# Attention and gated linear unit: the scheduler's transfers gated, and one causal select per chunk for both heads

## The chip, the cores and the metric

One core of one Trainium2 chip. The metric is the device time of one execution in microseconds. Most executions of a kernel lie in a fast state; some take over 1.5% more than the fastest and are called slow. Verdicts use fast runs alone. The span of a profiled run is the time from its first to its last instruction.

## The reference

Eight sequences of 576 tokens, 8 heads of 64. Causal attention with a decay bias from `s`, then a gated linear unit: a causal convolution of five taps makes the gate, and two 512x512 products make value and output.

```python
scores = scale * q @ k.T + minimum(-(cum_i - cum_j), 0)   # cum = cumsum(relu(s)); causal mask
x      = softmax(scores) @ v                              # (B, S, 512)
gate   = sigmoid(sum_k conv_w[k] * x shifted by (4 - k) tokens)
out    = (gate * (x @ w_val)) @ w_out
```

## The kernel before

A chunk is two heads of one batch: 4 chunks a batch, 32 in all. For each: transposes of q and k on TensorE, copies to `QKT`, scores, three exponentials of 128x1024 on ScalarE into `P`, the causal select of the diagonal blocks on GpSimd, A x V on TensorE, normalisation on VectorE, a transpose to `xT`, four taps of the convolution, tanh, value product, glu. At the end of each batch come five output products, each copied from PSUM into an `ot` tile and stored.

No engine runs this in program order. A list scheduler inside the kernel decides, when the kernel is built, the order in which each engine's instructions are emitted, from a price in microseconds for every task, and each engine then works through its list in order: in the profile of before GpSimd stands idle for up to 3.3 us before a select, with other work behind it in its list. The prices are literals in the code. These parts matter here:

```python
plan = Plan(dict(P=3, gp=2, th=6, ot=3, qkf=3))         # buffers of each pool

def mask(n, hh):                                        # one head's four diagonal blocks
    d = slot["Pt", n][:, hh, 0:512].rearrange("k (g q) -> k g q", g=4)
    nc.gpsimd.affine_select(out=d, in_=d, pattern=[[0, 4], [1, 128]], compare_op=ALU.is_ge, fill=0.0, base=0,
                            channel_multiplier=-1)

def tap(e, n, sh):                                      # one tap: two instructions on GpSimd, one on VectorE
    ...
    if e == "POOL":
        nc.gpsimd.tensor_tensor(tmp[:, o:S], xs[:, 2 - sh + o:2 - sh + S], r.to_broadcast([128, S - o]), ALU.mult)
        nc.gpsimd.tensor_tensor(gp[:, o:S], tmp[:, o:S], gp[:, o:S] if o else xs[:, 2:], ALU.add)
    elif o:
        nc.vector.scalar_tensor_tensor(gp[:, o:S], slot["x", n][:, 0:S - o], r, gp[:, o:S], ALU.mult, ALU.add)
...
# prices: exponential 0.905, select 0.6 each, a tap 0.73 on VectorE or 2.25 on GpSimd
t = add("ACT", 0.905, n + 0.3 * i, lambda n=n, i=i: exps(n, i), [t], give=[("pair", ("s", n, i))])
es += [t] if i else [add("POOL", 0.6, n + due("mask") + 0.01 * hh, lambda n=n, hh=hh: mask(n, hh), [t])
                     for hh in range(2)]
...
t = add(("DVE", "POOL"), (0.73, 2.25), n + due("tap") + sh * due("dtap"), lambda e, n=n, sh=sh: tap(e, n, sh), ...)
```

Of the kernel before, what the change touches and what calls it, by code (L numbers as in the profile page):

```python
# [14 lines left out]
ALU = mybir.AluOpType  # L15
# [190 lines left out]
def pcol(kb, qb):  # L206
    if kb == qb:
        return kb * 128
    if qb == 4:
# [16 lines left out]
DUE = dict(w=-69.33, lwv=-4.26, lwo=-2.61, cwv=56.85, cwo=86.75, av=-11.07, norm=-74.98, xt=-16.64,  # L226
           xe=-86.49, tap=14.23, dtap=-1.47, tanh=-72.16, val=7.76, dval=0.88, out=11.28, dout=0.61,
           oute=87.55, qt=-4.79, qe=133.25, tt=-0.4, te=-149.08, s4=-20.03, vp=-7.1, cast=76.15, lqk=-1.56,
           mask=-123.76, lv=-49.38, av_e=7.71, av_l=6.68, cast_e=-31.51, cast_l=0.54, dout_e=-1.01,
           dout_l=-28.82, dtap_e=-7.57, dtap_l=16.17, dval_e=0.26, dval_l=0.84, lqk_e=-7.13, lqk_l=48.32,  # L230
           lv_e=98.37, lv_l=-92.01, mask_e=11.67, mask_l=11.41, norm_e=50.24, norm_l=38.99, out_e=0.39,
           out_l=42.92, oute_e=70.67, oute_l=-23.24, qe_e=-66.52, qe_l=-3.56, qt_e=4.39, qt_l=0.95,
           s4_e=8.96, s4_l=-14.16, tanh_e=58.9, tanh_l=56.45, tap_e=3.56, tap_l=-27.97, te_e=47.36,
           te_l=62.72, tt_e=19.75, tt_l=0.79, val_e=-3.44, val_l=-1.96, vp_e=-68.8, vp_l=29.32, xe_e=13.94,
           xe_l=0.22, xt_e=-5.82, xt_l=-13.61)


def due_of(b, name):
# [5 lines left out]
STAY = (0.1, 54.75)  # L244

CHOICE = dict(vp0="0100",
              cast="12200210",
              wts="00",
              te="10001100",
              qe="10100010000000001000100000100010",  # L250
              xe="00100010001000010000000000010010",
              tap="00000000100000000000001000000000000000010000100000000000000010000000000000001000001000001000100000000010000010010010001101110000",
              oute="1000001110101000010100010100011010000010")


class Plan:
# [22 lines left out]
    def run(self):  # L279
        engs = ["SP", "POOL", "PE", "ACT", "DVE"]  # L280
        free = {k: [(0.0, i) for i in range(n)] for k, n in self.bufs.items()}
        bank = [0.0] * 8
# [30 lines left out]
        while len(self.order) < len(self.tasks):  # L313
            started, later = False, []
            for e in engs:
# [36 lines left out]
                if e == "SP":  # L352
                    idle_at[e] = now + 0.06
                    dma_free = max(dma_free, now + 1.2) + us
                    t["done"] = dma_free + 0.8
                else:
                    idle_at[e] = t["done"] = now + us
# [21 lines left out]
def main_path(ctx, tc, q, k, v, s, moe_w_val, moe_conv_w, moe_w_out, out, okcnt):  # L379
# [9 lines left out]
    plan = Plan(dict(P=3, gp=2, th=6, ot=3, qkf=3))  # L389
# [81 lines left out]
    t = add("DVE", 0.65, -8, relu, [t_s])  # L471
    t = add("DVE", 1.3, -8, total, [t])
    t = add("DVE", 0.75, -8, centre, [t])
# [20 lines left out]
    t = add("SP", 0.3, -8.95, lambda: nc.sync.dma_start(out=cw, in_=moe_conv_w))  # L494
    t = add("PE", 0.3, -6, conv_T, [t], take=[("bank", "cw")])
# [11 lines left out]
    t_cw = add("DVE", 1.2, -6, ratios, [t], give=[("bank", "cw")])  # L507
# [9 lines left out]
    def cast_qk(eng, b, which, hs, f):  # L517
        eng(qkbs[which][b % 2].rearrange("p j (h d) -> p h j d", h=8)[:, hs],  # L518
                        f.rearrange("p h (j d) -> p h j d", j=4))
# [76 lines left out]
    def mask(n, hh):  # L596
        d = slot["Pt", n][:, hh, 0:512].rearrange("k (g q) -> k g q", g=4)
        nc.gpsimd.affine_select(out=d, in_=d, pattern=[[0, 4], [1, 128]], compare_op=ALU.is_ge, fill=0.0, base=0,  # L598
                                channel_multiplier=-1)
# [82 lines left out]
    for b in range(B):  # L682
# [4 lines left out]
        if b == 0:  # L687
            t_tl = add("SP", 1.45, -8.4, lambda: load_tail(0))
            t_tail = T["tailc", 0] = add("DVE", 0.45, -6, lambda: nc.vector.tensor_copy(tailbs[0], tails[0]), [t_tl])
            for p in range(4):  # L690
                for wh in range(2):
# [3 lines left out]
                    t = add("SP", 0.82, -8.5 + 0.5 * p + wh * 0.01, ld)  # L695
# [178 lines left out]
```

## Time and profile before

| | before |
|---|---|
| time, median of the 3 fast runs (range) | 211.16 us (209.36 to 211.21) |
| span of the profiled run | 209.3 us |
| first exponential of batch 1 | 31.8 us |
| last tap on GpSimd ends / TensorE ends / last copy ends | 195.8 / 201.8 / 204.0 us |

The prediction below shows the busy shares, the stretches, GpSimd's waits and the end. The groups of GpSimd's selects and tap halves are the ones to compare with the prices. They are from the view of groups by line; after the bar stand the busy time in us and the mean of one in ns, then the idle time before them:

```profile
L598 POOL TENSOR_SCALAR_AFFINE_SELECT P<-P 128x512 bf16<-128x512 bf16 x64 | 39.6, 640 | 11.3 <-ACT P L592 11.1
L644 POOL TENSOR_TENSOR tmp<-xT,ratio 128x576 f32<-128x576 bf16 (+3 forms) x18 | 20.6, 1142 | 1.0 <-ACT xT L635 0.5 <-DVE xT L635 0.2
L645 POOL TENSOR_TENSOR gp<-tmp,gp 128x573 f32<-128x573 f32 (+2 forms) x11 | 15.7, 1428 | 3.1 <-DVE gp L647 2.3
L645 POOL TENSOR_TENSOR gp<-tmp,xT 128x576 f32<-128x576 f32 x7 | 9.7, 1379 | 0.5
```

A select costs 0.64 us against a price of 0.6: right. A tap pair costs (20.6 + 15.7 + 9.7) / 18 = 2.56 us against 2.25: 0.3 too cheap, 18 times. The chain that ended last, by engine, has no GpSimd compute in it:

```profile
DVE 27%; ACT 24%; PE 23%; DMA 8%; issue 8%; SPq 7%; ACTq 0%; DVEq 0%
```

### The profile page before, as it was taken

The page shows a single profiled execution, that of the slowest core. Times are in us where ns is not written, and L with a number is a line of the kernel's source. Part 1 is how long each engine was busy: PE and PEld are TensorE (multiplying, and loading weights), DVE is VectorE, ACT ScalarE, POOL GpSimd, SP SyncE. Part 2 cuts the span into 40 slices and gives each one's busy share as a digit, 9 for nine tenths or more (in the row PEclk, how much of TensorE's full clock was granted, in tenths as well). Part 3 has the DMA queues.
Part 4 walks back from the last instruction along what each step waited for, and adds up shares of the span by engine and source line. Part 5 has one row for each costly group of instructions (what it writes and reads, how often), then busy time and mean ns, then how long its engine had stood idle before and what let it go on. Part 6 is the DMA issues. An engine that isn't in the chain of part 4 may idle for free.

```text
span 209.3 us, 6007 instructions
## 1 busy us (share of the span) xinstructions
PE 175.4 (84%) x2392; PEld 119.4 (57%) x2411; DVE 178.0 (85%) x311; ACT 163.1 (78%) x205; POOL 161.9 (77%) x179
## 2 busy tenths in 40 slices
PE   1697885999969998689899799989899999979950
PEld 0455763475736766367665567565576556645620
DVE  3847969999888998669999999999999998999810
ACT  3279497778999899987996998799987998553330
POOL 4276486499959998999589999967975899999300
PEclk9999797599999999999999999999999999999995
DMA  4999999997999699999999821951149220222551
GB/s 147 238 279 288 361 147 216 354 271 207 244 281 323 138 319 221 323 297 226 222 383 307 190 107 25 184 147 49 54 110 219 81 77 1 99 104 75 180 180 61
DMA packets 69230, 40.48 MB, mean 193 GB/s; under 512 B 47109, under 2 KB 63493, under 8 KB 69194
## 3 DMA queue, kind: packets, MB, share of 16 engines
q1 hardware_dynamic: 69194, 40.01, 72.7%
q8 instruction: 21, 0.34, 0.7%
q14 instruction: 15, 0.12, 0.2%
HBM read 30.57 MB, written 9.44 MB: 191 GB/s over the span
## 4 chain that ended last, share of the span: by engine, by line
DVE 27%; ACT 24%; PE 23%; DMA 8%; issue 8%; SPq 7%; ACTq 0%; DVEq 0%
ACT P L592 13%; DVE gp L647 9%; PE banks L660 8%; DMA qkf<-in_moe_w_val_dram 6%; PE banks L672 6%; DVE xn L623 4%; PE banks L613 4%; ACT QKT L561 4%; ACT th L653 4%; DVE glu L666 3%; DVE gp L649 3%; PE banks L566 3%; SPq L515 3%; SPq L534 2%; ACT ot L677 2%
## 5 line engine op out<-in xcount | busy, mean ns | idle before, releaser
L592 ACT ACTIVATE P<-banks 128x1024 bf16<-128x1024 f32 x96 | 94.8, 1039 | 11.8 <-PE banks L566 9.9
L647 DVE SCALAR_TENSOR_TENSOR gp<-banks,ratio,gp 128x574 f32<-128x574 bf16 (+2 forms) x85 | 67.5, 804 | 2.4 <-POOL gp L645 1.7
L598 POOL TENSOR_SCALAR_AFFINE_SELECT P<-P 128x512 bf16<-128x512 bf16 x64 | 39.6, 640 | 11.3 <-ACT P L592 11.1
L566 PE MATMUL banks<-QKT 64*128 64x128 bf16 (+4 forms) x576 | 38.9, 249 | 8.8 <-ACT P L592 5.6
L660 PE MATMUL banks<-xT,wv 128*128 128x288 bf16 x256 | 41.7, 294 | 2.1 <-DVE glu L666 0.9
L672 PE MATMUL banks<-wo,glu 128*128 128x512 bf16 x141 | 38.3, 379 | 2.5 <-ACT QKT L561 0.8
L528 POOL TENSOR_TENSOR Vp<-vst,w 128x650 bf16<-128x650 f32 x29 | 37.6, 1316 | 1.3 <-DMA vst<-in_v_dram 1.3
L613 PE MATMUL banks<-Vp,P 128*128 128x65 bf16 x960 | 37.3, 198 | 1.3 <-ACT P L592 1.2
L613 PEld LDWEIGHTS <-P 128*128 128x128 bf16 x960 | 35.3, 101 | 5.4 <-issue 2.1
L566 PEld LDWEIGHTS <-QKT 64*128 64x128 bf16 x576 | 20.1, 97 | 27.0 <-issue 20.6
L653 ACT ACTIVATE th<-gp,halfw 128x576 f32<-128x576 f32 x32 | 25.2, 793 | 7.1 <-DVE gp L647 3.6
L660 PEld LDWEIGHTS <-wv 128*128 128x128 bf16 x256 | 22.8, 99 | 13.9 <-issue 6.1
L666 DVE SCALAR_TENSOR_TENSOR glu<-th,banks 128x288 bf16<-128x288 f32 x64 | 28.0, 445 | 1.1 <-PE banks L660 1.0
L623 DVE TENSOR_TENSOR xn<-banks,recs 128x640 bf16<-128x640 f32 x32 | 26.2, 818 | 0.3
L561 ACT COPY QKT<-banks 128x1024 bf16<-128x1024 bf16 x25 | 25.3, 1049 | 1.2 <-PE banks L557 1.1
L677 ACT COPY ot<-banks 128x512 f32<-128x512 f32 (+1 forms) x26 | 15.2, 587 | 11.4 <-PE banks L672 6.9
L672 PEld LDWEIGHTS <-glu 128*128 128x128 bf16 x160 | 14.6, 97 | 15.5 <-issue 2.7
L649 DVE SCALAR_TENSOR_TENSOR gp<-xT,ratio,banks 128x576 f32<-128x576 bf16 x25 | 20.1, 809 | 1.6 <-ACT xT L635 0.9
L644 POOL TENSOR_TENSOR tmp<-xT,ratio 128x576 f32<-128x576 bf16 (+3 forms) x18 | 20.6, 1142 | 1.0 <-ACT xT L635 0.5
L645 POOL TENSOR_TENSOR gp<-tmp,gp 128x573 f32<-128x573 f32 (+2 forms) x11 | 15.7, 1428 | 3.1 <-DVE gp L647 2.3
L631 PE MATMUL banks<-ident,xn 128*128 128x128 bf16 x160 | 14.2, 220 | 2.9 <-DVE xn L623 1.2
L518 POOL CAST qb<-qkf 128x2048 bf16<-128x2048 f32 x7 | 13.2, 1890 | 2.2 <-DMA qkf<-in_q_dram 2.2
(63 smaller groups left out, 169.2 us busy)
## 6 DMA issues: line engine op xcount, KB each, us to landing
out_dram<-ot SPq DMA_DIRECT2D x32, 256.0 KB, 2.9
qkf<-in_q_dram SPq DMA_DIRECT2D x7, 1024.0 KB, 8.5
qkf<-in_k_dram SPq DMA_DIRECT2D x7, 1024.0 KB, 9.9
vst<-in_v_dram SPq DMA_DIRECT2D x28, 256.0 KB, 5.4
vst<-in_v_dram SPq DMA_DIRECT2D x15, 128.0 KB, 4.0
first<-in_q_dram SPq DMA_DIRECT2D x4, 256.0 KB, 3.4
first<-in_k_dram SPq DMA_DIRECT2D x4, 256.0 KB, 3.4
tail<-in_q_dram SPq DMA_DIRECT2D x8, 128.0 KB, 8.7
```

Source lines behind the costliest of these rows:

```text
L528: eng.tensor_tensor(Vps[b % 2][:, :, h], vst[:, :, h], w[:, :, b * 8 + 2 * p:b * 8 + 2 * p + 2].unsqueeze(3).to_broadcast([128, NKB, 2, 65 ...
L561: copy[e](QKTs[b % 2][:, :, p, 0:512].rearrange("d w (x j) -> d w x j", j=4), slot["qt", b, p].rearrange("d w (j x) -> d w x j", j=4))
L566: nc.tensor.matmul(ps[:, hh, c0:c0 + nq], QKTs[b % 2][r, 1, p, k0:k0 + 128], QKTs[b % 2][r, 0, p, q0:q0 + nq], **kw)
L592: nc.scalar.activation(out=slot["Pt", n][:, :, step * 512:(step + 1) * 512], in_=slot["s", n, step], func=AF.Exp, scale=0.125)
L598: nc.gpsimd.affine_select(out=d, in_=d, pattern=[[0, 4], [1, 128]], compare_op=ALU.is_ge, fill=0.0, base=0, channel_multiplier=-1)
L613: nc.tensor.matmul(ps[:, hh, qb * 65:qb * 65 + 65], lhsT, Vps[b % 2][:, kb, 2 * p + hh, :], start=(kb == 0), stop=(kb == qb))
L623: nc.vector.tensor_tensor(xns[b % 2][:, :, p * 128:(p + 1) * 128].rearrange("t g (h d) -> t h g d", h=2), pv[:, :, :, 0:64], recs[:, n].un ...
L647: nc.vector.scalar_tensor_tensor(gp[:, o:S], slot["x", n][:, 0:S - o], r, gp[:, o:S], ALU.mult, ALU.add)
L653: nc.scalar.activation(out=th, in_=slot["g", n], func=AF.Tanh, scale=halfw[:, n % 4, :])
L660: nc.tensor.matmul(ps, wv[:, dc, c * 128:(c + 1) * 128], xTs[b % 2][:, dc, 2 + o:290 + o], start=(dc == 0), stop=(dc == 3))
L666: nc.vector.scalar_tensor_tensor(glus[b % 2][:, c, o], slot["t", n][:, o], 1.0, slot["v", n, hf], ALU.add, ALU.mult)
L672: nc.tensor.matmul(ps, glus[b % 2][:, c, WIN[i]:WIN[i] + 128], wo[:, c, :], start=(c == 0), stop=(c == 3))
```

## The change

Two changes of the kernel and one of the scheduler's picture. One select of 1024 elements for both heads, priced at 0.75 us, takes the place of two of 512. `ot` gets five buffers in place of three. In the scheduler, a transfer may be issued no sooner than 11.48 us before the queue is thought free ("gating"; nothing on the chip waits for it). Then the keys (the scheduler's priorities) and engine choices were searched anew, so the order on all engines is another one.

```diff
-STAY = (0.1, 54.75)
-CHOICE = dict(vp0="0100", cast="12200210", ... )
+STAY = (1.35, 151.9)
+BEHIND = 11.48
+CHOICE = dict(tailc="2", vp0="1100", cast="00112001", ... )        # and all of DUE
 ...
                 if e == "SP":
-                    idle_at[e] = now + 0.06
                     dma_free = max(dma_free, now + 1.2) + us
+                    idle_at[e] = max(now + 0.06, dma_free - BEHIND)
 ...
-    plan = Plan(dict(P=3, gp=2, th=6, ot=3, qkf=3))
+    plan = Plan(dict(P=3, gp=2, th=6, ot=5, qkf=3))
 ...
-    def mask(n, hh):
-        d = slot["Pt", n][:, hh, 0:512].rearrange("k (g q) -> k g q", g=4)
-        nc.gpsimd.affine_select(out=d, in_=d, pattern=[[0, 4], [1, 128]], compare_op=ALU.is_ge, fill=0.0, base=0,
+    def mask(n):
+        d = slot["Pt", n][:, :, 0:512].rearrange("k h (g q) -> k h g q", g=4)
+        nc.gpsimd.affine_select(out=d, in_=d, pattern=[[0, 2], [0, 4], [1, 128]], compare_op=ALU.is_ge, fill=0.0, base=0,
                                 channel_multiplier=-1)
 ...
-                es += [t] if i else [add("POOL", 0.6, n + due("mask") + 0.01 * hh, lambda n=n, hh=hh: mask(n, hh), [t])
-                                     for hh in range(2)]
+                es += [t] if i else [add("POOL", 0.75, n + due("mask"), lambda n=n: mask(n), [t])]
```

The rest of the diff gives the first batch's loads, casts and transposes keys of their own in place of fixed ones.

More of the change, by code (lines that the diff above doesn't have):

```diff
@@ L222 @@
 NEG = -30000.0
-DUE = dict(w=-69.33, lwv=-4.26, lwo=-2.61, cwv=56.85, cwo=86.75, av=-11.07, norm=-74.98, xt=-16.64,
-           xe=-86.49, tap=14.23, dtap=-1.47, tanh=-72.16, val=7.76, dval=0.88, out=11.28, dout=0.61,
-           oute=87.55, qt=-4.79, qe=133.25, tt=-0.4, te=-149.08, s4=-20.03, vp=-7.1, cast=76.15, lqk=-1.56,
-           mask=-123.76, lv=-49.38, av_e=7.71, av_l=6.68, cast_e=-31.51, cast_l=0.54, dout_e=-1.01,
-           dout_l=-28.82, dtap_e=-7.57, dtap_l=16.17, dval_e=0.26, dval_l=0.84, lqk_e=-7.13, lqk_l=48.32,
-           lv_e=98.37, lv_l=-92.01, mask_e=11.67, mask_l=11.41, norm_e=50.24, norm_l=38.99, out_e=0.39,
-           out_l=42.92, oute_e=70.67, oute_l=-23.24, qe_e=-66.52, qe_l=-3.56, qt_e=4.39, qt_l=0.95,
-           s4_e=8.96, s4_l=-14.16, tanh_e=58.9, tanh_l=56.45, tap_e=3.56, tap_l=-27.97, te_e=47.36,
-           te_l=62.72, tt_e=19.75, tt_l=0.79, val_e=-3.44, val_l=-1.96, vp_e=-68.8, vp_l=29.32, xe_e=13.94,
-           xe_l=0.22, xt_e=-5.82, xt_l=-13.61)
+DUE = dict(w=-179.07, lwv=6.9, lwo=25.99, cwv=119.71, cwo=21.81, av=-67.91, norm=-106.36, xt=-83.29,
+           xe=-39.43, tap=73.53, dtap=-12.21, tanh=-21.14, val=7.28, dval=1.38, out=12.56, dout=0.92,
+           oute=44.7, qt=-5.37, qe=224.11, tt=0.85, te=-141.54, s4=-66.86, vp=-112.81, cast=107.85,
+           lqk=56.02, mask=-117.33, lv=13.25, av_e=68.91, av_l=-46.36, cast_e=-153.69, cast_l=-53.98,
+           dout_e=-12.2, dout_l=-66.84, dtap_e=-10.04, dtap_l=-64.5, dval_e=14.84, dval_l=-0.73,
+           lqk_e=-53.46, lqk_l=16.33, lv_e=84.68, lv_l=-81.16, mask_e=2.46, mask_l=30.46, norm_e=62.66,
+           norm_l=45.33, out_e=82.66, out_l=-73.32, oute_e=83.06, oute_l=-53.09, qe_e=-68.49, qe_l=46.96,
+           qt_e=-24.08, qt_l=3.94, s4_e=27.55, s4_l=-86.7, tanh_e=20.1, tanh_l=94.17, tap_e=-15.62,
+           tap_l=-2.33, te_e=-55.59, te_l=-34.48, tt_e=-48.5, tt_l=-36.85, val_e=-96.42, val_l=2.31,
+           vp_e=-46.58, vp_l=160.49, xe_e=32.24, xe_l=-1.61, xt_e=14.3, xt_l=-78.88, sd=-18.85, lcw=-44.05,
+           cvt=23.68, rat=-67.55, lt0=-98.57, tailc0=29.75, lq0=-12.67, lq0d=2.97, cast0=-5.61,
+           cast0d=127.18, lv0=-3.45, lv0d=2.76, vp0=32.35, vp0d=-5.83, tt0=62.96, te0=134.74, qt0=19.06,
+           qe0=-26.31, q0d=25.23)
@@ L238, in due_of @@
 def due_of(b, name):
     return DUE[name] + (DUE[name + "_e"] if b < 2 else DUE[name + "_l"] if b > 5 else 0)
-STAY = (0.1, 54.75)
-CHOICE = dict(vp0="0100",
-              cast="12200210",
-              wts="00",
-              te="10001100",
-              qe="10100010000000001000100000100010",
-              xe="00100010001000010000000000010010",
-              tap="00000000100000000000001000000000000000010000100000000000000010000000000000001000001000001000100000000010000010010010001101110000",
-              oute="1000001110101000010100010100011010000010")
+STAY = (1.35, 151.9)
@@ L256 @@
+BEHIND = 11.48
+CHOICE = dict(tailc="2",
+              vp0="1100",
+              cast="00112001",
+              wts="00",
+              te="00000100",
+              qe="01110110001000001001110000100100",
+              xe="01111000001011110000000100100111",
+              tap="00000000100001000000000100010000010000001100000000000010100000001000011000000010000100010000010010000110000100000100010010110000",
+              oute="0010011001000000110010100000000010001100")
 class Plan:
@@ L469, in decay_T @@
             nc.tensor.transpose(pt[:, i, :], cum[:, WIN[i]:WIN[i] + 128], identf)
-    t = add("DVE", 0.65, -8, relu, [t_s])
-    t = add("DVE", 1.3, -8, total, [t])
-    t = add("DVE", 0.75, -8, centre, [t])
+    t = add("DVE", 0.65, DUE["sd"], relu, [t_s])
+    t = add("DVE", 1.3, DUE["sd"], total, [t])
+    t = add("DVE", 0.75, DUE["sd"], centre, [t])
     t = add("PE", 1.2, DUE["w"], decay_T, [t], take=[("bank", "w")])
@@ L492, in conv_T @@
             nc.tensor.transpose(pt[:, c, :], cw[:, c * 128:(c + 1) * 128], identf[0:5, 0:5])
-    t = add("SP", 0.3, -8.95, lambda: nc.sync.dma_start(out=cw, in_=moe_conv_w))
-    t = add("PE", 0.3, -6, conv_T, [t], take=[("bank", "cw")])
+    t = add("SP", 0.3, DUE["lcw"], lambda: nc.sync.dma_start(out=cw, in_=moe_conv_w))
+    t = add("PE", 0.3, DUE["cvt"], conv_T, [t], take=[("bank", "cw")])
     def ratios():
@@ L505, in ratios @@
         nc.vector.tensor_scalar(ok[:, NS * NKB * 2:], sq, 1e20, None, ALU.is_le)
-    t_cw = add("DVE", 1.2, -6, ratios, [t], give=[("bank", "cw")])
+    t_cw = add("DVE", 1.2, DUE["rat"], ratios, [t], give=[("bank", "cw")])
     T = {}
@@ L687, in main_path @@
         if b == 0:
-            t_tl = add("SP", 1.45, -8.4, lambda: load_tail(0))
-            t_tail = T["tailc", 0] = add("DVE", 0.45, -6, lambda: nc.vector.tensor_copy(tailbs[0], tails[0]), [t_tl])
+            t_tl = add("SP", 1.45, DUE["lt0"], lambda: load_tail(0))
+            t_tail = T["tailc", 0] = add(("DVE", "ACT", "POOL"), (0.45, 0.48, 0.7), DUE["tailc0"], lambda e: copy[e](
+                tailbs[0], tails[0]), [t_tl], pick=("tailc", 0))
             for p in range(4):
@@ L694, in ld @@
                         dma_qk(0, wh, HP[p], f)
-                    t = add("SP", 0.82, -8.5 + 0.5 * p + wh * 0.01, ld)
-                    T["cast", 0, wh, p] = add(("DVE", "ACT", "POOL"), (0.32, 0.5, 0.8), p - 9, lambda e, p=p, wh=wh: cast_qk(
+                    t = add("SP", 0.82, DUE["lq0"] + DUE["lq0d"] * p + wh * 0.01, ld)
+                    T["cast", 0, wh, p] = add(("DVE", "ACT", "POOL"), (0.32, 0.5, 0.8), DUE["cast0"] + p * DUE["cast0d"], lambda e, p=p, wh=wh: cast_qk(
                         copy[e], 0, wh, HP[p], slot["f", 0, wh, p]), [t], pick=("cast", 2 * p + wh))
-                t = add("SP", 1.45, -8.3 + 0.5 * p, lambda p=p: load_v_pair(p))
-                T["vp", 0, p] = add(("DVE", "POOL"), (0.85, 1.25), p - 2, lambda e, p=p: vprime(
+                t = add("SP", 1.45, DUE["lv0"] + DUE["lv0d"] * p, lambda p=p: load_v_pair(p))
+                T["vp", 0, p] = add(("DVE", "POOL"), (0.85, 1.25), DUE["vp0"] + p * DUE["vp0d"], lambda e, p=p: vprime(
                     nc.vector if e == "DVE" else nc.gpsimd, 0, p), [t, t_w], pick=("vp0", p))
@@ L722, in main_path @@
         old_s = ([T.get(("s4", b - 2, 3))] + [T.get(("s", n0 - 8 + p, i)) for p in range(4) for i in range(3)])
-        t = T["tt", b] = add("PE", 0.25, n0 + due("tt") if b else -6.5, lambda b=b: tail_T(b), [t_tail] + old_s,
+        t = T["tt", b] = add("PE", 0.25, n0 + due("tt") if b else DUE["tt0"], lambda b=b: tail_T(b), [t_tail] + old_s,
                              take=[("bank", ("tt", b))])
-        t_te = add(("ACT", "DVE"), (0.49, 0.6), n0 + due("te") if b else -6.3, lambda e, b=b: tail_evac(e, b), [t],
+        t_te = add(("ACT", "DVE"), (0.49, 0.6), n0 + due("te") if b else DUE["te0"], lambda e, b=b: tail_evac(e, b), [t],
                    give=[("bank", ("tt", b))], pick=("te", b))
         for p in range(4):
-            t = T["qt", b, p] = add("PE", 0.45, n0 + p + due("qt") if b else p - 6.9, lambda b=b, p=p: qk_T(b, p),
+            t = T["qt", b, p] = add("PE", 0.45, n0 + p + due("qt") if b else DUE["qt0"] + p * DUE["q0d"], lambda b=b, p=p: qk_T(b, p),
                                     [T["cast", b, 0, p], T["cast", b, 1, p]] + old_s, take=[("bank", ("qt", b, p))])
-            T["qe", b, p] = add(("ACT", "DVE"), (0.9, 1.15), n0 + p + due("qe") if b else p - 6.8,
+            T["qe", b, p] = add(("ACT", "DVE"), (0.9, 1.15), n0 + p + due("qe") if b else DUE["qe0"] + p * DUE["q0d"],
                                 lambda e, b=b, p=p: qk_evac(e, b, p), [t], give=[("bank", ("qt", b, p))], pick=("qe", n0 + p))
```

## The prediction

> **What bounds the kernel now.** I read the page's busy shares first, then the table of stretches, the groups, the waits, the time-ordered view of GpSimd and of the last microseconds.
>
> The busy shares say that no engine is the bound alone:
>
> ```profile
> PE 175.4 (84%) x2392; PEld 119.4 (57%) x2411; DVE 178.0 (85%) x311; ACT 163.1 (78%) x205; POOL 161.9 (77%) x179
> ```
>
> The table of three stretches (start-up, middle, tail) shows where the remaining idle time lies: columns are PE, PEld, DVE, ACT, POOL busy us with counts, then clock, DMA share, GB/s.
>
> ```profile
> 0.00:40.00 40.00, 27.42 (x341) 19.59 (x341) 29.13 (x49) 26.29 (x35) 23.87 (x41) 0.89 0.97 249
> 40.00:180.00 140.00, 127.47 (x1905) 87.83 (x1921) 130.46 (x230) 127.33 (x156) 123.16 (x127) 1.00 0.75 192
> 180.00:209.00 29.00, 20.52 (x154) 11.98 (x152) 18.39 (x34) 9.46 (x15) 14.91 (x12) 0.93 0.36 125
> ```
>
> In the middle 140 us DVE is 93% busy, PE and ACT 91%, GpSimd 88%: four engines in one pipeline, each nearly full. Work taken from one and given to another pays only if the receiver has room. GpSimd has the most, and the view of waits says for what it stands still:
>
> ```profile
> POOL P L598 <- ACT P L592: 11.1, 11, 3.3
> POOL P L603 <- ACT P L578: 7.3, 5, 2.5
> ```
>
> These are the causal selects that come before the exponentials have delivered; they were put early in GpSimd's order.
>
> The end of the run, in order of time, is a shortage of buffers. Columns: start, duration, engine, line, what, and idle time before it with its releaser:
>
> ```profile
> 197.74 4.05 PE L672 MATMUL banks<-wo,glu 128*128 128x512 bf16 x17
> ...
> 201.08 0.59 ACT L677 COPY ot<-banks 128x512 f32<-128x512 f32 x1 [1.26 <-DMA out_dram<-ot]
> 203.44 0.59 ACT L677 COPY ot<-banks 128x512 f32<-128x512 f32 x1 [1.77 <-DMA out_dram<-ot]
> ```
>
> TensorE is done at 201.79, but the last two copies out of PSUM wait for a store to free one of three `ot` buffers; the last copy ends at 204.03.
>
> **What the Trainium skill says.** First, "GPSIMD Engine Reference", section 3.1: a GpSimd core runs a software loop whose bound is the number of elements, plus a dispatch for each instruction. The trace agrees for the select: 128 elements a partition take 0.31 us, 512 take 0.63, so about 0.84 ns for each element more. Second, "TensorE: Matmul & The Clock Gate", Architectural detail: ScalarE, VectorE and GpSimd are strict FIFO. So a kernel's emitted order is what counts, and a late GpSimd instruction delays all behind it; nothing in the trace contradicts that. Third, "DMA: Bandwidth & Descriptors", section on the SWDGE path: a wait for a semaphore happens on the issuing sequencer before dispatch, not in the DMA engines. The trace shows the same side of it: one queue on SyncE issues all, one after another, 0.4 to 0.7 us each from 0.81 to 16.5 us, and later a group of five loads takes 6.67 us to issue. Fourth, "SBUF — State Buffer", Who interferes with whom: a VectorE instruction in a two-port mode and GpSimd block each other. One case fits it: a GpSimd tap half that takes 1.38 us on average took 2.06 beside VectorE's 128x2048 weight cast.
>
> **The change part by part.** The kernel is emitted by a small list scheduler at build time. "Gating" changes only that scheduler's picture of the transfer queue (it no longer believes that it can issue every 0.06 us without limit); no wait is added on the chip. With it come new priorities and new engine choices, so the whole order moves. I counted instructions of each kind in both orders and multiplied by the mean durations of the groups.
>
> VectorE: 5 more QKT copies (1.217 us each, +6.1), 2 fewer small ones (0.42, -0.8), 3 fewer output copies (0.68, -2.1), 8 fewer xT copies (0.451, -3.6), 7 fewer taps (0.805, -5.6), 1 fewer Vp product (-0.8), casts about level. Sum -6.8: 178.0 becomes 171.
>
> ScalarE: 5 fewer QKT copies (1.049, -5.2), 2 more small ones (+1.2), 1 more cast (+0.6), 3 more output copies (+1.8), 8 more xT copies (0.664, +5.3). Sum +3.7: 163.1 becomes 167.
>
> GpSimd: 64 selects of 512 elements become 32 of 1024. A pair took 1.23 us back to back, so 64 cost 39.4. One of 1024 by the slope above is 0.63 + 512 x 0.84 ns = 1.06 us, 32 cost 34: -5.4. The scheduler is told 0.75 us; the trace gives me no reason to believe that, since only the fixed 0.2 us is saved, not half. Tap pairs rise from 18 to 25; a pair is 1.14 + 1.42 us: +17.9. One Vp product more (+1.3), casts net one fewer (-0.6). Sum +13.2: 161.9 becomes 175.
>
> TensorE: the same instructions, 175.4.
>
> The four together go from 678 to 688 us. So the gain cannot come from less work; it must come from less waiting.
>
> On the path that sets the end: **the tail.** The pool of `ot` buffers grows from 3 to 5, so the last copy can start at about 201.85 and end at 202.44 in place of 204.03: -1.6 us, the one item I am sure of.
>
> **The head.** Before, the first q/k and v loads alternate; after, all q/k of the first batch come first and the v loads behind them. Exponentials of batch 0 can follow each other with fewer gaps (ScalarE idles 4.4 of the 20 us from 10 to 30). But the first exponential gets no earlier (the tail loads come first now), and batch 1 waits for the same bytes: DMA share is 1.03 and 1.08 in these two slices. I give it -1 us.
>
> **GpSimd's line.** From the first select of batch 1 (at 33.65 us before) GpSimd has, before: 12 casts x 1.85, 28 products x 1.26, 7 small selects x 0.62, 5 tail casts x 0.57, 17 tap pairs x 2.62, 56 selects x 0.615 = 143.7 us (start to start durations). It ends its last tap at 195.77, so it idled 18.4 us. After: seven tap pairs more (+18.3) and 28 selects x 1.07 for 56 x 0.615 (-4.5): 157.5 us. With the same start its last tap ends at 191.2 plus its idle time, then tanh, glu, the last 20 output matmuls, a copy and a store: 195.77 to 209.3 is 13.5 us before, 11.9 with the buffers. Time over span is 1.7 us (211.03 against 209.3). So the time is at least 33.7 + 157.5 + 11.9 + 1.7 = 204.8 us plus GpSimd's idle time after batch 1 starts. An engine with 10 us more to do than its planner believes runs late, and a late engine seldom waits: I take 3 us of idle. That makes **207.8 us**.
>
> **The rivals.** One: GpSimd becomes the bound and makes others wait. For it: the sum above, 28 selects each 0.3 us dearer than the scheduler believes (8.9 us), and the matmuls that need the masked P. If 7 us of idle remain, the time is 212, no gain. Against it: the search that chose the new order may have had slack there, and batch 7 has less left on GpSimd (21 us of work from its first select, against 31.5). Two: VectorE was the real bound at 93%, its 6.8 us come off, and a better order of transfers closes gaps as well: 211.2 - 1.6 - 1 - 5 = 203.6. Against it: VectorE's relief is GpSimd's load. Three: the select of 1024 elements really costs 0.75 us; then GpSimd has 149 us after batch 1 and is no bound, 204 to 206. The 512-element group speaks against it. Four: transfers are hidden anyway (their share falls to 0.1 to 0.7 after 120 us) and their new order does nothing; then only tail and balance remain, about 209.
>
> **Range and chances.** The rivals span 203.6 to 212 and the runs before themselves 209.4 to 211.2. I set 203 to 213. Faster by 2% needs below 206.9; it needs rival two or three, or nearly no idle on GpSimd: 0.40. Within 2%: 0.54. Slower: 0.06, if GpSimd's lateness runs through everything.
>
> **What would show it.** Selects: a group of 32 with a mean of 1.03 to 1.10 us. GpSimd busy 173 to 177, VectorE 170 to 173, ScalarE 165 to 168. GpSimd's wait for the exponentials falls from 18 us to below 8. More of TensorE's and ScalarE's waits name GpSimd. The last copies wait for TensorE, none for a store. The middle stretch shows GpSimd at 94% or more. I am wrong if GpSimd still waits over 10 us for exponentials while the time falls below 206 (then batch 1 starts earlier, or the select is cheap), or if GpSimd is busy all through and the time is above 213.

## The result

| | before | after |
|---|---|---|
| time, median of 4 (range; 212.93 was a slow run) | 211.19 us (209.36 to 212.93) | 217.0 us (216.85 to 217.32) |
| span of the profiled run | 209.3 us | 215.1 us |

The ratio is 1.0307 (95% interval 1.0241 to 1.0373): slower by 3.1%. Ratios here are the mean time of one kernel's fast runs over that of the other's of the same rounds, so not quite the ratio of the medians.

Busy shares and chain of the kernel after. The forecasts of busy time came right (GpSimd 173 to 177, VectorE 170 to 173, ScalarE 165 to 168), and GpSimd, absent from the chain before, is now its largest part:

```profile
PE 176.6 (82%) x2394; PEld 120.2 (56%) x2411; DVE 172.8 (80%) x295; ACT 166.0 (77%) x214; POOL 177.0 (82%) x161
...
POOL 31%; PE 20%; DVE 13%; issue 13%; ACT 12%; SPq 4%; DMA 3%; POOLq 0%; DVEq 0%; ACTq 0%
```

GpSimd's groups of after. The select is 1.10 us, as forecast, not 0.75; 25 tap pairs cost (28.6 + 26.8 + 7.2) / 25 = 2.50 us each, not 2.25:

```profile
L604 POOL TENSOR_SCALAR_AFFINE_SELECT P<-P 128x1024 bf16<-128x1024 bf16 x32 | 35.1, 1099 | 5.1 <-ACT P L598 4.8
L650 POOL TENSOR_TENSOR tmp<-xT,ratio 128x574 f32<-128x574 bf16 (+3 forms) x25 | 28.6, 1146 | 2.8 <-ACT xT L641 2.2
L651 POOL TENSOR_TENSOR gp<-tmp,gp 128x574 f32<-128x574 f32 (+2 forms) x19 | 26.8, 1413 | 3.7 <-DVE gp L653 2.4
L651 POOL TENSOR_TENSOR gp<-tmp,xT 128x576 f32<-128x576 f32 x6 | 7.2, 1203 | 0.5
```

The table of stretches of after (columns as in the prediction). In the middle 140 us GpSimd is busy 134.2 us (96%; before 123.2), VectorE has fallen from 130.5 to 121.2, TensorE from 127.5 to 124.4:

```profile
0.00:40.00 40.00, 24.84 (x333) 18.61 (x334) 27.67 (x43) 25.93 (x36) 24.12 (x35) 0.95 0.94 248
40.00:180.00 140.00, 124.41 (x1791) 84.88 (x1803) 121.20 (x210) 121.61 (x153) 134.22 (x112) 0.96 0.71 192
180.00:215.00 35.00, 27.39 (x277) 16.67 (x277) 23.91 (x45) 18.43 (x27) 18.63 (x16) 0.98 0.30 105
```

Some of the waits of after (total us, times, longest). GpSimd waits less: its two waits for exponentials, 18.4 us before, are 7.0. VectorE's taps wait 5.5 us for it (before 1.7) and A x V 3.9 (before, for no select that the list shows). The lines of PEld and PE are two views of the same stalls, so 3.5 and 2.8 must not be added: the four stalls end at 19.1, 28.3, 125.9 and 179.3 us and make 3.9 us. ScalarE's tanh, which waited 3.3 us for GpSimd before, waits for it no longer. Together: 5.0 us before, 9.4 after.

```profile
DVE gp L653 <- POOL gp L651: 5.5, 7, 1.5
POOL P L604 <- ACT P L598: 4.8, 4, 2.5
PEld L619 <- POOL P L604: 3.5, 3, 1.5
PE banks L619 <- POOL P L604: 2.8, 4, 1.3
...
POOL P L609 <- ACT P L584: 2.2, 2, 1.2
```

and those of before that are named above:

```profile
ACT th L653 <- POOL gp L645: 3.3, 3, 2.0
...
DVE gp L647 <- POOL gp L645: 1.7, 2, 1.5
```

The end of after, in order of time. No copy waits for a store any more; the last copy comes 0.6 us after the last matmul, where it came 2.2 us after it before:

```profile
201.50 3.11 PE L666 MATMUL banks<-xT,wv 128*128 128x288 bf16 x24
204.45 4.48 PE L678 MATMUL banks<-wo,glu 128*128 128x512 bf16 x19
...
208.96 0.59 ACT L683 COPY ot<-banks 128x512 f32<-128x512 f32 x1 [1.10 <-PE banks L678]
```

So where did 5.8 us of span come from? Cut each trace at two events, the first exponential of batch 1 and the end of the last copy:

| kernel | to batch 1 | batch 1 to last copy | rest of span |
|---|---|---|---|
| before | 31.8 | 172.2 | 5.3 |
| after | 36.0 | 173.5 | 5.6 |

By this count 4.2 us come from the start-up and only 1.3 from all that follows. But the part that follows should have become shorter: five buffers and the searched order were there to shorten it. Two questions for the chip, then: what made batch 1 late, and what ate the gain behind it.

### The profile page after: what moved, and what is told of

The parts are those of the page before. It is cut to its first block, busy times and chain, and to the rows that moved or that the text cites. A ratio compares the mean times of both kernels' runs of the same rounds, so it can differ in the third digit from the quotient of the medians.

```text
span 215.1 us, 5995 instructions
## 1 busy us (share of the span) xinstructions
PE 176.6 (82%) x2394; PEld 120.2 (56%) x2411; DVE 172.8 (80%) x295; ACT 166.0 (77%) x214; POOL 177.0 (82%) x161
## 4 chain that ended last, share of the span: by engine, by line
POOL 31%; PE 20%; DVE 13%; issue 13%; ACT 12%; SPq 4%; DMA 3%; POOLq 0%; DVEq 0%; ACTq 0%
POOL Vp L534 8%; POOL gp L651 7%; POOL tmp L650 7%; ACT P L598 6%; PE banks L619 6%; PE banks L678 5%; PE banks L666 5%; POOL P L604 5%; DVE gp L653 3%; DVE xn L629 3%; DMA first<-in_k_dram 2%; DVE glu L672 2%; PE banks L572 2%; PE banks L563 2%; SPq L540 2%
## 5 line engine op out<-in xcount | busy, mean ns | idle before, releaser
L653 DVE SCALAR_TENSOR_TENSOR gp<-banks,ratio,gp 128x572 f32<-128x572 bf16 (+2 forms) x77 | 61.3, 804 | 6.2 <-POOL gp L651 5.5
L666 PE MATMUL banks<-xT,wv 128*128 128x288 bf16 x256 | 40.5, 296 | 1.9 <-DVE gp L653 1.2
L619 PEld LDWEIGHTS <-P 128*128 128x128 bf16 x960 | 35.7, 102 | 11.4 <-issue 3.7
L534 POOL TENSOR_TENSOR Vp<-vst,w 128x650 bf16<-128x650 f32 x30 | 39.0, 1321 | 1.8 <-ACT w L481 1.8
L604 POOL TENSOR_SCALAR_AFFINE_SELECT P<-P 128x1024 bf16<-128x1024 bf16 x32 | 35.1, 1099 | 5.1 <-ACT P L598 4.8
L572 PEld LDWEIGHTS <-QKT 64*128 64x128 bf16 x576 | 18.9, 97 | 27.2 <-issue 20.1
L650 POOL TENSOR_TENSOR tmp<-xT,ratio 128x574 f32<-128x574 bf16 (+3 forms) x25 | 28.6, 1146 | 2.8 <-ACT xT L641 2.2
L666 PEld LDWEIGHTS <-wv 128*128 128x128 bf16 x256 | 23.3, 100 | 13.3 <-issue 6.8
L651 POOL TENSOR_TENSOR gp<-tmp,gp 128x574 f32<-128x574 f32 (+2 forms) x19 | 26.8, 1413 | 3.7 <-DVE gp L653 2.4
L683 ACT COPY ot<-banks 128x512 f32<-128x512 f32 (+1 forms) x29 | 17.1, 599 | 9.7 <-PE banks L678 7.2
L567 ACT COPY QKT<-banks 128x1024 bf16<-128x1024 bf16 x20 | 20.0, 1024 | 4.8 <-PE banks L563 4.8
L637 PE MATMUL banks<-ident,xn 128*128 128x128 bf16 x160 | 14.1, 219 | 3.2 <-DVE xn L629 2.0
L567 DVE COPY QKT<-banks 128x1024 bf16<-128x1024 bf16 x12 | 14.4, 1216 | 2.6 <-PE banks L563 2.6
```

The costliest lines, as they stand in the source:

```text
L534: eng.tensor_tensor(Vps[b % 2][:, :, h], vst[:, :, h], w[:, :, b * 8 + 2 * p:b * 8 + 2 * p + 2].unsqueeze(3).to_broadcast([128, NKB, 2, 65 ...
L567: copy[e](QKTs[b % 2][:, :, p, 0:512].rearrange("d w (x j) -> d w x j", j=4), slot["qt", b, p].rearrange("d w (j x) -> d w x j", j=4))
L572: nc.tensor.matmul(ps[:, hh, c0:c0 + nq], QKTs[b % 2][r, 1, p, k0:k0 + 128], QKTs[b % 2][r, 0, p, q0:q0 + nq], **kw)
L604: nc.gpsimd.affine_select(out=d, in_=d, pattern=[[0, 2], [0, 4], [1, 128]], compare_op=ALU.is_ge, fill=0.0, base=0, channel_multiplier=-1)
L619: nc.tensor.matmul(ps[:, hh, qb * 65:qb * 65 + 65], lhsT, Vps[b % 2][:, kb, 2 * p + hh, :], start=(kb == 0), stop=(kb == qb))
L666: nc.tensor.matmul(ps, wv[:, dc, c * 128:(c + 1) * 128], xTs[b % 2][:, dc, 2 + o:290 + o], start=(dc == 0), stop=(dc == 3))
```

## The experiments

All keep every engine's emitted order of the kernel that they start from, unless the text says otherwise, so that a difference is the cost or the wait that was changed and not another plan. Names with `a_` start from after, with `b_` from before. Fifteen kernels ran. The medians are of all runs of a kernel, slow ones too; the ratios, against before on the same chip, are of fast runs alone. The cuts are those of the table above, from each profile. Among the profiles of before and of the b_ runs in the fast state the start of batch 1 varies from 30.6 to 31.8, so half a microsecond in that column means little.

| run | median us | ratio, 95% | to batch 1 | batch 1 to last copy | GpSimd busy |
|---|---|---|---|---|---|
| after | 217.0 | 1.031 [1.024, 1.037] | 36.0 | 173.5 | 177.0 |
| a_two | 219.95 | 1.041 [1.034, 1.049] | 36.5 | 176.4 | 181.4 |
| a_cheap | 211.36 | 1.005 [1.003, 1.008] | 35.6 | 168.0 | 164.5 |
| a_tapcheap | 211.66 | 1.006 [1.004, 1.008] | 37.0 | 167.7 | 168.7 |
| a_bothcheap | 208.34 | 0.990 [0.980, 1.000] | 35.7 | 166.0 | 157.1 |
| a_taps | 213.99 | 1.019 [1.015, 1.022] | (slow profile) | | 159.2 |
| b_one | 211.34 | 1.002 [0.999, 1.006] | 31.2 | 172.4 | 156.6 |
| b_slow | 213.43 | 1.021 [1.015, 1.027] | 31.4 | 173.5 | 170.9 |
| b_ot5 | 208.2 | 0.989 [0.984, 0.994] | 30.6 | 169.9 | 161.4 |
| a_ot3f | 228.97 | 1.095 [1.088, 1.101] | 36.3 | 183.6 | |
| b_all | 208.3 | 0.988 [0.984, 0.991] | (slow profile) | | |
| a_sp | 216.5 | 1.025 [1.018, 1.032] | 35.8 | 173.7 | 175.4 |
| a_actq | 215.8 | 1.023 [1.016, 1.030] | 35.4 | 173.5 | 175.2 |
| a_kb | 217.23 | 1.038 [1.034, 1.041] | 35.5 | 173.5 | 176.0 |
| a_start | 217.58 | 1.033 [1.022, 1.045] | 36.3 | 173.9 | 176.0 |
| a_startcheap | 209.97 | 0.999 [0.996, 1.001] | 34.9 | 166.5 | 155.9 |

### First theory: GpSimd carries more than its prices say

**a_cheap**: the select at its price. It covers 640 elements, so the output is wrong on purpose.

```diff
-        d = slot["Pt", n][:, :, 0:512].rearrange("k h (g q) -> k h g q", g=4)
-        nc.gpsimd.affine_select(out=d, in_=d, pattern=[[0, 2], [0, 4], [1, 128]], ...
+        d = slot["Pt", n][:, :, 0:320]
+        nc.gpsimd.affine_select(out=d, in_=d, pattern=[[0, 2], [1, 320]], ...
```

> Changed kernel, every engine's order kept, but the select works on 640 elements a partition in place of 1024 (wrong output on purpose), so that it costs about the 0.75 us that the scheduler was told in place of the measured 1.10. That is 32 x 0.35 = 11 us off GpSimd. Theory 1 (GpSimd's own line of work sets the time): 217.0 falls to 206 to 209, that is by most of the 11 us, until another engine binds. Theory 2 (the new order of start-up and the moved copies cost the time, GpSimd is only busy): stays at 215 to 217.

211.36 us, 2.6% of before's time below after (1.031 to 1.005). That lies between the ranges of the two theories. The part behind batch 1 shrinks by 5.5 us, the start-up by 0.4. The middle stretch of a_cheap and its waits, where after's were 124.41 and 134.22 busy, and 5.5, 3.5 and 2.8 of waiting for GpSimd:

```profile
40.00:180.00 140.00, 127.80 (x1876) 86.71 (x1890) 125.15 (x217) 125.72 (x159) 130.27 (x116) 0.99 0.73 196
```

```profile
POOL P L604 <- ACT P L598: 7.8, 7, 2.9
...
DVE gp L653 <- POOL gp L651: 2.5, 5, 0.9
PEld L619 <- POOL P L604: 2.5, 2, 1.3
PE banks L619 <- POOL P L604: 0.9, 1, 0.9
PEld L619 <- POOL P L609: 0.9, 1, 0.9
```

The other engines get more done in the same 140 us and wait less for GpSimd (the taps 2.5 us in place of 5.5, A x V 3.3 for the selects in place of 3.9, each stall counted once): 12.5 us less of GpSimd's work gave about 5.5 us of time.

**a_two**: the opposite, two selects of 512 at the place of one.

```diff
-        d = slot["Pt", n][:, :, 0:512].rearrange("k h (g q) -> k h g q", g=4)
-        nc.gpsimd.affine_select(out=d, in_=d, pattern=[[0, 2], [0, 4], [1, 128]], ...
+        for hh in range(2):
+            d = slot["Pt", n][:, hh, 0:512].rearrange("k (g q) -> k g q", g=4)
+            nc.gpsimd.affine_select(out=d, in_=d, pattern=[[0, 4], [1, 128]], ...
```

> Changed kernel, order kept, the two selects of 512 of before at the place of the one of 1024. A pair costs 1.23 us back to back, the one 1.06 to 1.10: 32 x 0.15 = 4 to 5 us more on GpSimd. Theory 1: 220 to 222. Theory 2: 217.

219.95 us. 4.4 us more of GpSimd's busy time cost 2.9 us behind batch 1 (1.0% by the ratios, about 2.1 us of time). So the slope is alike on both sides: 0.5 to 0.7 us of time here, 0.44 in a_cheap, for one of GpSimd's work.

**a_tapcheap** and **a_bothcheap**: the taps nearer their price, on fewer columns, alone and with the cheap select (wrong on purpose).

```diff
+    nc.vector.memset(tmp, 0.0)
 ...
+            f, f2 = (S - 88, S - 88) if o else (S - 176, S)
-            nc.gpsimd.tensor_tensor(tmp[:, o:S], xs[:, 2 - sh + o:2 - sh + S], r.to_broadcast([128, S - o]), ALU.mult)
-            nc.gpsimd.tensor_tensor(gp[:, o:S], tmp[:, o:S], gp[:, o:S] if o else xs[:, 2:], ALU.add)
+            nc.gpsimd.tensor_tensor(tmp[:, o:f], xs[:, 2 - sh + o:2 - sh + f], r.to_broadcast([128, f - o]), ALU.mult)
+            nc.gpsimd.tensor_tensor(gp[:, o:f2], tmp[:, o:f2], gp[:, o:f2] if o else xs[:, 2:], ALU.add)
```

> After, with GpSimd's taps on fewer columns (wrong result on purpose; order kept; tmp set to zero by VectorE at the start so that nothing unset is read). A pair should fall from about 2.52 us to about 2.2 us, near the 2.25 us that the scheduler was told, so GpSimd's busy time falls by about 8 to 9 us from 177. Theory (GpSimd carries more than the scheduler was told, and half of it comes out in the time, as with the cheap select): 212 to 214 us, and the lag from batch 1 to the end grows by about 2 us in place of 4.5. Rival (only the select's price matters, because A x V waits for it, the taps are off the path): unchanged, 216 to 217.

> After, cheap taps and the cheap select of 640 elements together (wrong result on purpose). GpSimd then costs about what the scheduler was told. Theory: the two savings overlap, 207 to 209.5 us; the lag behind the plan stays at 4 to 5 us from batch 1 on and shrinks, as only the start-up's loss is left. Rival (once GpSimd has slack another engine is the bound, so the second saving brings nothing): as with the cheap select alone, 211 to 212.

211.66 us for the taps alone, though nothing of the select was touched: the rival that only the select's price matters falls. (Its output passed the comparison, which shows only that the comparison is coarse for the gate.) GpSimd's busy time fell by 8.3 us, the part behind batch 1 by 5.8. Both together: 208.34 us, the part behind batch 1 shorter by 7.5. The savings overlap (5.5 and 5.8 alone) but do not stop at one of them, so the second rival falls too. With the select at 0.75 us and a pair at (24.0 + 23.2 + 7.2) / 25 = 2.18 us, both near their prices (the groups of a_bothcheap, then its chain by engine), GpSimd has left the chain that ended last:

```profile
L652 POOL TENSOR_TENSOR tmp<-xT,ratio 128x486 f32<-128x486 bf16 (+3 forms) x25 | 24.0, 962 | 5.0 <-ACT xT L642 3.4 <-DVE xT L642 1.0
L605 POOL TENSOR_SCALAR_AFFINE_SELECT P<-P 128x640 bf16<-128x640 bf16 x32 | 23.8, 746 | 11.0 <-ACT P L599 10.9
L653 POOL TENSOR_TENSOR gp<-tmp,gp 128x486 f32<-128x486 f32 (+2 forms) x19 | 23.2, 1221 | 4.2 <-DVE gp L655 3.0
L653 POOL TENSOR_TENSOR gp<-tmp,xT 128x576 f32<-128x576 f32 x6 | 7.2, 1203 | 0.5
```

```profile
PE 37%; ACT 24%; DVE 22%; issue 9%; DMA 3%; SPq 2%; POOL 0%; DVEq 0%; ACTq 0%
```

This is the central result: what these two kinds of instruction cost above their prices makes about 4% of before's time in the order of after (1.031 to 0.990), more than the whole loss. It does not show a gain in the new order. The 1% below before rests on four runs, and the interval reaches 1.000; and **b_ot5**, below, gets 0.989 from the old order at real costs by its five `ot` buffers alone, which after has too. Nor was a search run with the right prices: that the wrong prices led the search to this order is likely, but not shown.

**a_taps**: the load taken off in a correct kernel, seven tap pairs moved to VectorE when emitted.

```diff
+MOVED = {(6, 4), (8, 2), (13, 3), (16, 1), (17, 3), (21, 4), (25, 2)}
-                t = add(("DVE", "POOL"), (0.73, 2.25), ..., lambda e, n=n, sh=sh: tap(e, n, sh),
+                t = add(("DVE", "POOL"), (0.73, 2.25), ..., lambda e, n=n, sh=sh: tap("DVE" if (n, sh) in MOVED else e, n, sh),
```

> Changed kernel, seven tap pairs of batches 1 to 6 given back to VectorE at their place in the order (25 pairs become 18, as before the change): 7 x 2.6 = 18 us off GpSimd, 7 x 0.8 = 5.6 us on VectorE. Theory 1: 207 to 210, held up by the start-up that is 3.7 us later. Theory 2: 214 to 217.

213.74 us is the median of the fast runs, 1.2% below after by the ratios. That misses the 207 to 210 expected of theory 1 and a_tapcheap's mark, though GpSimd was relieved by 17.8 us. A possible reason, not tested: VectorE's seven taps come at places in its list that were planned without them. Its profile fell in the slow state, so I read nothing finer from it.

**b_slow**: does before's order have room on GpSimd? A superfluous select of 128 elements for each chunk.

```diff
     def mask(n, hh):
         ...
+        if hh:
+            d = slot["Pt", n][:, hh, 0:128]
+            nc.gpsimd.affine_select(out=d, in_=d, pattern=[[1, 128]], compare_op=ALU.is_ge, fill=0.0, base=0,
+                                    channel_multiplier=-1)
```

> Kernel before, order kept, one superfluous select of 128 elements (about 0.29 us, the output stays right) after each pair: 32 x 0.29 = 9.3 us more for GpSimd, which has 19 us of idle time after the start-up. Theory 3 (the changed order is hurt since GpSimd has no idle time left): 0 to 3 us more, 211 to 214. If GpSimd's work counts in any order by half or more (as from 0.74 to 1.10 us a select in the changed order: 5.4 us for 11): 5 us more or above, 216.

9.0 us more of GpSimd's work cost 2.1%, 3.6 us by the medians of the fast runs (b_slow's profiled run is its fastest and shows 1.1 us of span). So even with 12% idle in the middle stretch that engine has little free room: its idle time stands in front of exponentials, and in a fixed order it cannot be moved to where work is late. Idle time is not slack.

### The parts of the change alone

**b_one**: the merged select in before, at the first head's place.

```diff
     def mask(n, hh):
-        d = slot["Pt", n][:, hh, 0:512].rearrange("k (g q) -> k g q", g=4)
-        nc.gpsimd.affine_select(out=d, in_=d, pattern=[[0, 4], [1, 128]], ...
+        if hh:
+            return
+        d = slot["Pt", n][:, :, 0:512].rearrange("k h (g q) -> k h g q", g=4)
+        nc.gpsimd.affine_select(out=d, in_=d, pattern=[[0, 2], [0, 4], [1, 128]], ...
```

> Kernel before, order kept, one select of 1024 elements at the place of the first of each pair, none for the second: 32 x 0.15 = 4 to 5 us off GpSimd. Where GpSimd is not the bound (it idles 19 us after 33 us): within 0.7% of before. If GpSimd's work counts everywhere as in the changed kernel (about 0.5 to 0.7 us of time for each us of its work): 1 to 1.4% faster.

211.34 us, ratio 1.002: nothing. The group of b_one, against 64 x 640 ns before:

```profile
L600 POOL TENSOR_SCALAR_AFFINE_SELECT P<-P 128x1024 bf16<-128x1024 bf16 x32 | 34.9, 1093 | 15.1 <-ACT P L592 14.1 <-DMA vst<-in_v_dram 0.9
```

Merging saves 39.6/32 - 34.9/32 = 0.15 us of busy time a chunk, and it goes into waiting: the wait for exponentials rises from 11.1 to 14.1 us. In before's order the merged select is neither a gain nor a loss: 5.3 us less of GpSimd's work gave nothing there, though 9.0 us more (b_slow) cost 2.1%.

**b_ot5** and **a_ot3f**: the buffers alone, `ot` tiles used in turn, five in before's order and three in after's.

```diff
+    ots = []
-        ot = slot["ot", b, i] = work("ot", (b, i), [128, DM], FP32)
+        ots.append(0)
+        ot = slot["ot", b, i] = one.tile([128, DM], FP32, name=f"ot{len(ots) % 5}")   # % 3 in a_ot3f
```

> Kernel before, order kept, five output buffers in turn in place of three. The last copy waited 1.77 us for a store, the one before 1.26: 1.5 us less, 0.7% faster. If the last store's landing or the check of the records sets the end: the same time.

> Changed kernel, order kept, three output buffers in turn in place of five. If the buffers give in the changed kernel what they gave before (209.3 to 205.9 span there, of which 1.6 us at the last copies): 218.5 to 219.5. If the changed order has room for the stores: 217.

b_ot5 takes 208.2 us, 1.1% less than before, with a correct result: **it beats both kernels**, and it is one number in the source. (The verdict is still "same", as 1.1% is less than 2%; but the interval excludes 1.) Its last copies, to be held against before's, which waited 1.26 and 1.77 us for a store:

```profile
199.03 0.59 ACT L680 COPY ot<-banks 128x512 f32<-128x512 f32 x1 [1.10 <-PE banks L672]
199.89 0.59 ACT L680 COPY ot<-banks 128x512 f32<-128x512 f32 x1 [0.28 <-PE banks L672]
```

From the last matmul (199.9) to the last copy's end (200.5) are 0.6 us in place of 2.2: the 1.6 us that the prediction was sure of. In after's order five buffers are not a gain but a need; with three the copies wait for stores (a_ot3f's waits on ScalarE; with VectorE's, three in the middle, from 68 to 98 us, and two after 217 us), and the time is 229 us, ten above what was expected:

```profile
ACT ot L686 <- DMA out_dram<-ot: 10.3, 3, 4.8
```

**b_all**: before with the merged select, five `ot` tiles in turn and the loads of `s` and of the first tails on ScalarE's queue.

```diff
-    t_s = add("SP", 0.8, -9, lambda: nc.sync.dma_start(out=sp, in_=s.rearrange("b h s -> (b h) s")))
+    t_s = add("SP", 0.8, -9, lambda: nc.scalar.dma_start(out=sp, in_=s.rearrange("b h s -> (b h) s")))
-            nc.sync.dma_start(out=tails[b % 2][r, :]...
+            (nc.sync if b else nc.scalar).dma_start(out=tails[b % 2][r, :]...
```

> Kernel before, order kept, with the select merged, five output buffers and the tail and s loads on ScalarE's queue: the sum of what the single changes give, 2 to 5 us faster than before if all count (205 to 208), 209 if only the buffers do.

208.3 us (208.1 by the fast runs), as b_ot5. The other two parts add nothing that can be measured.

### The start-up: five attempts

Batch 1 starts 4.2 us later in after. These are the first lines of GpSimd's list there, in order of time:

```profile
27.15 1.10 POOL L604 TENSOR_SCALAR_AFFINE_SELECT P<-P 128x1024 bf16<-128x1024 bf16 x1 [1.49 <-ACT P L598]
28.20 1.89 POOL L524 CAST kb<-qkf 128x2048 bf16<-128x2048 f32 x1
...
37.40 1.10 POOL L604 TENSOR_SCALAR_AFFINE_SELECT P<-P 128x1024 bf16<-128x1024 bf16 x1
```

and in before:

```profile
25.77 1.89 POOL L518 CAST kb<-qkf 128x2048 bf16<-128x2048 f32 x1 [0.80 <-DMA qkf<-in_k_dram]
27.61 1.23 POOL L598 TENSOR_SCALAR_AFFINE_SELECT P<-P 128x512 bf16<-128x512 bf16 x2
...
33.65 1.23 POOL L598 TENSOR_SCALAR_AFFINE_SELECT P<-P 128x512 bf16<-128x512 bf16 x2
```

The cast of batch 1's k ran ahead of batch 0's last select before, and runs behind it now. Other suspects: `s` is loaded later (the first V' product then waits 1.83 us for `w`), and the tail loads go first on the queue.

**a_sp**, the load of `s` first; **a_actq**, tails and `s` on ScalarE's queue (the edit of b_all); **a_kb**, the k cast ahead of the last select:

```diff
-        for t in plan.order:
+        for t in [t_s] + [t for t in plan.order if t is not t_s]:          # a_sp
             t["emit"]()
```

```diff
+        order = list(plan.order)                                           # a_kb
+        kb = next(t for t in order if t is T["cast", 1, 1, 0])
+        late = next(i for i, t in enumerate(order) if t is t_m3)           # batch 0's last select
+        order.remove(kb)
+        order.insert(late, kb)
+        for t in order:
-        for t in plan.order:
             t["emit"]()
```

> Changed kernel, only the load of s moved to the front of the queue, all else in the same order. It is needed for the decay factors, these for the scaled V and these for the first A x V. In the changed kernel the first A x V starts at 19.1 us against 15.4 before and batch 1's first select at 37.4 against 33.65. Theory 1: the select comes 1 to 3 us earlier and the time falls by as much, 214 to 216. A theory that the start-up is the whole loss: 212 to 213.

> Changed kernel, with the first three loads (both tails of batch 0, and s) issued from ScalarE's queue, which is idle until 6 us, so that SyncE's first q and k loads are issued about 2 us earlier; all else in the same order. In the changed kernel the first exponential of batch 1 starts at 36.0 us against 31.8 before. Theory 3 (two losses add: about 2 to 4 us of start-up, and about 5 us by which GpSimd falls behind later): batch 1 starts 1 to 3 us earlier and the time falls by 1 to 3, to 214 to 216. Theory 1 (GpSimd's line alone): the same fall if its first select of batch 1 moves. If the time stays at 217 while batch 1 starts earlier, the start-up is hidden behind GpSimd.

> Changed kernel, two GpSimd instructions of the start-up exchanged: the cast of batch 1's k (28.20 us, 1.89 us long) goes ahead of the select of batch 0's last chunk, which waits 1.49 us for its exponential and holds the cast back; kernel before has them in this order (cast at 25.77). Everything else in the same order. If the late start of batch 1 (36.0 us against 31.8) comes from here and adds to the loss: batch 1's first exponential at 33.5 to 34.5 and 1.5 to 2.5 us less time, 214.5 to 215.5. If GpSimd's fullness later hides it: batch 1 earlier, time 217.

216.5, 215.8 and 217.23 us; batch 1 starts at 35.8, 35.4 and 35.5. In a_kb the cast of k starts at 25.84 us, as its load lands; before it did so at 25.77, so that load is not late in after. Neither the loads nor the cast alone are the cause. In a_kb TensorE's list still had A x V of batch 0's last chunk, which waits for that select, ahead of batch 1's transposes. So:

**a_start**: a_kb, and the four pairs of transposes ahead of that A x V. **a_startcheap**: the same with the cheap select and taps.

```diff
+        def ahead(t, of):
+            order.remove(t)
+            order.insert(order.index(of), t)
+        ahead(T["cast", 1, 1, 0], t_m3)
+        for p in range(4):
+            ahead(T["qt", 1, p], t_av3)
```

> After, with the cast of batch 1's first k ahead of the last select of batch 0 on GpSimd and the four pairs of batch 1's q/k transposes ahead of A x V of batch 0's last chunk on TensorE, the rest of the order kept (right result). Theory (batch 1 starts late because its transposes stand behind A x V, which waits for the last select of batch 0): batch 1's first exponential comes at 33 to 34.5 in place of 36.0, its first select with it, and as GpSimd has hardly any slack after it the time falls nearly as much: 214 to 215.5. Rival (the late start is given by the loads and by the slow casts before 20 us): start at 35.5 or later, time 216 to 217.

> After, with the start-up order of a_start and the cheap taps and select of a_bothcheap (wrong result on purpose). If start-up and GpSimd's load add up, the time is that of a_bothcheap less what a_start saves, about 205 to 207.5; if the pipeline catches up a late start whenever GpSimd has slack, it equals a_bothcheap within 0.7 us.

217.58 us, and batch 1 at 36.3: my theory of the start-up fell. TensorE in a_start, in order of time:

```profile
30.15 0.38 PE L563 MATMUL banks<-ident,qb 128*128 128x128 bf16 x4 [2.46 <-ACT P L598]
...
35.65 0.40 PE L572 MATMUL banks<-QKT 64*128 64x128 bf16 x8 [2.14 <-DVE gp L653]
```

The transposes moved ahead only to wait 2.46 us until ScalarE had emptied PSUM banks, and the first scores of batch 1 waited 2.14 us for a bank that a tap on VectorE held. The delay is spread over three engines' lists and the PSUM banks; none of the swaps tried takes it out. In a_startcheap the start comes 0.8 us earlier than in a_bothcheap and the part behind it is 0.5 us longer. It runs at 209.97 us, not the 205 to 207.5 expected if the two causes added; against a_bothcheap's four runs (ratio 0.990, interval to 1.000) it is rather slower than faster. What makes batch 1 late in after **stays open**, and as no experiment moved the start of after's order by more than 1.1 us, it is counted but not shown that those 4 us are part of the loss.

One thing seen there: TensorE ran slow just when batch 1's transposes came. Stretches from 30 to 34 us, after and then before; the third number from the end is the granted clock:

```profile
30.00:34.00 4.00, 4.00 (x60) 4.00 (x58) 3.08 (x6) 2.31 (x3) 2.27 (x3) 0.65 0.94 204
```

```profile
30.00:34.00 4.00, 1.71 (x27) 1.20 (x25) 4.00 (x6) 3.07 (x5) 3.92 (x5) 1.00 1.04 213
```

Four transposes took 0.63 us in after there and 0.39 us in before. In the 4 us ahead of them TensorE of after had been busy 1.84 us. That resembles the Trainium skill, "TensorE: Matmul & The Clock Gate", HAM oscillation, where pauses lower the clock of the work that follows; but its pauses are waits of 3 to 5 us, and the longest here was 1.25 us. In a_start they ran at 0.39 us, and nothing was gained, so this was no cause by itself.

## Why the prediction was wrong

The time was 217.0, above the range of 203 to 213. The prediction was a sum, and each term can be measured in the trace of after:

| term | predicted | measured | difference |
|---|---|---|---|
| batch 1's first select starts | 33.7 | 37.4 | +3.7 |
| GpSimd's work from there to its last tap | 157.5 | 156.9 | -0.6 |
| GpSimd's idle time in it (gaps over 0.15 us) | 3 | 7.5 | +4.5 |
| last tap to end of span | 11.9 | 13.3 | +1.4 |
| time over span | 1.7 | 1.75 | 0 |
| sum | 207.8 | 216.85 | +9.0 |

- **The costs were right.** The select at 1.06 (1.10 measured), the busy times of all engines, the -1.6 us of the buffers (b_ot5), the fall of GpSimd's wait for exponentials below 8 us (7.0), GpSimd above 94% in the middle (96%): all as foretold. Rival three, a select of 0.75 us, was rightly put aside; a_cheap shows what it would have been worth. Rival two, VectorE as the real bound, failed: VectorE had 5.2 us less to do, and the time rose. One sign came out half: TensorE's waits name GpSimd more often (3.9 us at A x V), ScalarE's less (the tanh's 3.3 us are gone).
- **The first step that failed**: "An engine with 10 us more to do than its planner believes runs late, and a late engine seldom waits: I take 3 us of idle." It waited 7.5 us, and this is the term that was off most. 4.7 of the 7.5 are two waits: 2.54 us at 167.4 for an exponential and 2.11 us at 197.7 for a tap on VectorE. A late engine waits little only if what it waits for comes on time. A reading that fits, though no run isolates it: the engines form a ring. A x V waits for the select and VectorE's taps wait for GpSimd's tap halves (9.4 us of such waits in after, 5.8 in a_cheap), and their lateness delays the exponentials and `xT` copies that GpSimd's next work needs. This is rival one, which I had put at 212 us with 7 us of idle: right in its idle time, and in its mechanism as far as the runs show it, short by the other two terms below.
- **The second**: "The head. [...] I give it -1 us." It was +3.7 (the sum left the start where it was, so the -1 never entered it). I had looked for gaps in ScalarE's list up to 30 us and for the bytes loaded, not at what the new order put between batch 0's last select and batch 1's first. Its cause stays open, as told.
- **The third**: the tail. The buffers gave their 1.6 us, but in after's order three chunks' value products (24 matmuls, 3.11 us) are left when the last tap ends, and TensorE is then busy 7.05 of 7.1 us; before it was 5.93 of 6.0. That is 1.1 of the 1.4.
- **The chances.** 0.06 for slower needed a reason why a shortfall of 10 us on GpSimd could not run through. b_slow shows that even the order before passes on over a third of such work, and a_cheap and a_two show 0.44 to 0.7 for after. The working had the number in it (8.9 us of dearer selects) and did not carry it into the time.

## What to carry to other kernels

A static plan relies on its prices: measure each kind of instruction in the profile of the kernel before, put that into the scheduler, and search only then. (Here this is advice: no such search was run.) The search gave the engine that was priced too low 15.1 us more to do and filled it to 96% of the middle stretch. When judging such a change blind, take (measured minus believed cost) times the count for every engine. In these runs 0.4 to 0.7 of the GpSimd work that was added or cut came out in the time, but 0.2 where it moved to VectorE (a_taps) and nothing in b_one. And try the small independent parts, here two more output buffers, on the old order first.

## What the Trainium skill lacked or had wrong

- "GPSIMD Engine Reference", 3.1, gives costs of tensor_tensor and says that the number of elements bounds the loop, which the runs bear out, but no cost of an affine select on bf16: here 0.31, 0.64 and 1.10 us for 128, 512 and 1024 elements a partition. Merging two of 512 saves 0.15 us of 1.24.
- "DMA: Bandwidth & Descriptors" gives a dispatch time for the path through GpSimd, but none that SyncE spends on issuing one transfer: 0.4 to 0.8 us each at the start of both kernels, one after another, where the kernel's scheduler believed 0.06.
- "SBUF — State Buffer", Who interferes with whom, says which instructions of VectorE and GpSimd block each other, but not how long a blocked select or cast takes: in the start-up of after a select of 128 elements took 0.49, 1.24 and 0.90 us in place of 0.31, and a 128x512 cast on GpSimd 1.62 in place of 0.63, beside casts, a scan and products of two tensors on VectorE. That fits the page; no run isolated it.
